# Top-32 attention into a mixture of experts: exponential before the mask, mask and product in one VectorE instruction

## The chip, the cores and the metric

The kernel runs on one NeuronCore of one Trainium2 chip. The metric is the device time of one launch in microseconds (us). A core has engines that run side by side, each with its own queue of instructions, executed in order: TensorE (PE in the profile; its weight loads are PEld), VectorE (DVE), ScalarE (ACT), GpSimd (POOL) and SyncE (SP, which issues transfers). An instruction that needs another engine's data waits on a semaphore, and all that stands behind it in its queue waits too.

## The reference

For 8 batches of 8 heads, 576 rows and head size 64, all in float32:

```python
scores = scale * np.matmul(q, k.transpose(0, 1, 3, 2))
kth = np.partition(scores, -32, axis=-1)[..., -32:-31]
scores = np.where(scores >= kth, scores, -1e9)
attn = np.exp(scores - scores.max(-1, keepdims=True))
attn = attn / (attn.sum(-1, keepdims=True) + 1e-9)
x = np.matmul(attn, v)
```

So each row of 576 scores keeps its 32 largest and takes a softmax over them. The result `x` (4608 rows of 512) goes through a mixture of 8 experts: each row is sent to one expert, two matrix products with a relu between them, and the result is scaled by the gate's probability.

## The kernel before

The attention is cut into 288 tiles of 128 rows by 576 scores: 32 pairs of heads, 9 tiles each. A loop over `i` runs one stage of several tiles in each pass, so that every engine has work of some tile. All engines get their instructions in the order in which the loop's Python code calls them; nothing reorders them later.

In pass `i` the stages of a tile `t` are these (the lag of a stage is the number of passes behind the tile's first stage on VectorE):

- TensorE computes the scores two passes ahead (`qk`), and ScalarE copies them from PSUM to SBUF as `Ssb` (`sevac`, L330).
- VectorE, lag 0: `subs` (L337), seven MAX8 over the seventh parts of a row, which gives 56 candidates. Lag 1: `chain` (L348 to L350), which takes the 24 largest of the candidates. `below` (L361) makes from the 24th a bound just under it.
- ScalarE, lag 3 (`KL + 1`): `sign` (L368) compares all scores with that bound. It writes the signs `K` and, with its accumulator, a sum `n` that tells how many scores lie above.
- GpSimd, lag 3: `pool_y` (L373) multiplies scores and signs to `y`, which hides the scores that are already counted.
- VectorE, lag 5 (`LT`): one MAX8 over the 576 values of `y` (L380) finds the next largest, and one scalar_tensor_tensor `jk` over 9 values (L381), by the count `n`, picks the 32nd largest, `kth`.
- VectorE, lag 5 (`LR`): `drop` (L387) writes `R`, which is 2 to the power 100 where a score is under `kth`, else 0.
- GpSimd, lag 6 (`LM`): `pool_m` (L392) subtracts `R` from the scores, giving `Sm`.
- ScalarE, lag 7 (`LE`): `expo` (L397) takes the exponential of `Sm` with the row's maximum subtracted, writes the probabilities `P` and their sum `den`.
- TensorE, lag 9 (`TL`): `trans` transposes `P`, ScalarE copies the result (`evac`), and TensorE multiplies with `v` (`av`).

VectorE's instructions of a pass come in three lists. `a_` holds the chain and `b_` the seven sub-maxima and the MAX8 over `y`; they are woven together. `c_` follows: `jk` (the pick), `below`, up to a few small instructions of routing and of the experts' scheduler ("side instructions" below; `small_` in the code), and `drop` last. TensorE fills its free time by a budget in the code (`STEP`, 3.2 us of estimated work a pass): what the attention leaves of it goes to matrix products of experts whose rows are ready. After the loop, from about 1100 us on, the remaining slots of the experts run alone.

GpSimd also does `small` (L356, the negated row maxima of three tiles), `fill` (L302, two copies each ninth pass), and the scattering transfers (L528, L718, L1088).

Of the kernel before, what the change touches and what calls it, by code (L numbers as in the profile page):

```python
# [19 lines left out]
TOPK = 32  # L20
NSUB = 7
CAP = 3.0
ME = 23
NB = 6
LX = 13
SN = 4
KB = 2
# [6 lines left out]
QL = 2  # L34
KW = 8
KL = 2
LT = KL + 3
LR = LT
LM = LR + 1
LE = LM + 1  # L40
TL = LE + 2
YB = 3
MB = 3
RB = 2
RL = (5, 6)
RX = (1, 3, 10, 12, 14)
HG = 2
# [6 lines left out]
QO = 0  # L54
# [7 lines left out]
BIG = float(2.0 ** 100)  # L62
# [7 lines left out]
def kernel(  # L70
# [35 lines left out]
    wk = att.enter_context(tc.tile_pool(name="wk", bufs=3))  # L106
# [5 lines left out]
    LD, PR, T = {}, {}, {}  # L112
    PAUSE = lambda: None

    def load(p, what, b=None):

        o = LD.setdefault(p, {})
        h0 = 2 * (p % HP)
        for nm in what:
            src = {"k": k, "q": q, "v": v}[nm]  # L120
            g = src[p // HP] if b is None else src[ds(b, 1)].rearrange("o h s d -> (o h) s d")
            t = ld.tile([128 if nm == "v" else 64, 2, D], FT, name=nm + "t", bufs=2 if nm == "v" else 1)
            m = ld.tile([128, 2, 4, D] if nm == "v" else [128, 4, 2, D], FT, name=nm + "m", bufs=2 if nm == "v" else 1)
# [25 lines left out]
    def fiota(name, shape, pattern, base, cm):  # L149
        t = const.tile(shape, FT, name=name)  # L150
        G.iota(t, pattern=pattern, base=base, channel_multiplier=cm, allow_small_or_imprecise_dtypes=True)
        return t

    i9s = fiota("i9s", [128, 9], [[2, 9]], S - 2 * TOPK, 0)
    ie = fiota("ie", [128, E], [[1, E]], -ZROW, 0)
    rev = fiota("rev", [128, E], [[-1, E]], E, 0)
    eoff = fiota("eoff", [128, E], [[LCAP, E]], -ZROW, 0)
# [15 lines left out]
    den = [const.tile([128, HP, 9], FT, name=f"den{i}") for i in range(2)]  # L173
    kth = const.tile([128, NT], FT, name="kth")
# [18 lines left out]
    x5 = const.tile([128, 5, XW], FT, name="x5")  # L193
# [25 lines left out]
    def bias_of(mw, mt, nb, bias):  # L219
        mf = wk.tile([128, nb, 5], FT, name="mf", bufs=1)  # L220
        G.memset(mf, 0.0)
        V.tensor_copy(mf[:, :, 0:4], mw[:, :, 0:8:2])
        V.tensor_copy(mf[:64, :, 4:5], mt[:, :, 0:1])
        nm = wk.tile([128, nb, 5], FT, name="nm", bufs=1)
        V.tensor_scalar(nm, mf, -1.0, 1.0, op0=OP.mult, op1=OP.add)
        tmp = wk.tile([128, nb, 5, E], FT, name="y", bufs=YB)
        bv = bias.rearrange("p b c e -> p (b c) e")
        tv = tmp.rearrange("p b c e -> p (b c) e")
        sh = [128, nb * 5, E]
        V.tensor_tensor(bv, mf.rearrange("p b c -> p (b c)")[:, :, None].to_broadcast(sh),  # L230
                        mbt[:, 1:2, :].to_broadcast(sh), op=OP.mult)
# [94 lines left out]
        T[i] = {"ps": ps}  # L326

    def sevac(i):
        T[i]["S"] = sb = wk.tile([128, S], FT, name="Ssb", bufs=LM + 1 + QL - QO)
        A.activation(sb.rearrange("p (a b) -> p a b", a=2), T[i]["ps"][:, :, :288], AF.Copy, scale=0.125)  # L330

    bnd = [(x * S) // NSUB for x in range(NSUB + 1)]
# [6 lines left out]
    def chain(i):  # L339
        if i % 3 == 0:  # L340
            T[i]["mg"] = wk.tile([128, 3, 32], FT, name="mg", bufs=5)
        else:
            T[i]["mg"] = T[i - 1]["mg"]
        m = T[i]["mg"][:, i % 3]
        c = T[i]["c"]
        c2 = wk.tile([128, NSUB * 8], FT, name="cand2", bufs=1)
        c3 = wk.tile([128, NSUB * 8], FT, name="cand3", bufs=1)
        return [lambda: V.max(m[:, 0:8], c), lambda: V.match_replace(c2, m[:, 0:8], c, -3e38),  # L348
                lambda: V.max(m[:, 8:16], c2), lambda: V.match_replace(c3, m[:, 8:16], c2, -3e38),
                lambda: V.max(m[:, 16:24], c3)]  # L350
# [6 lines left out]

    def below(i):
        t = T[i]
        t["n"] = wk.tile([128, 2], FT, name="n", bufs=NB)  # L360
        V.tensor_scalar(t["n"][:, 1:2], t["mg"][:, i % 3, 23:24], 1.0 - 2.0 ** -24, None, op0=OP.mult)  # L361

    def sign(i):


        t = T[i]
        t["K"] = wk.tile([128, S], BF, name="K", bufs=KB)
        A.activation(t["K"], t["S"], AF.Sign, scale=2.0 ** -24 - 1.0, bias=t["n"][:, 1:2], accum_out=t["n"][:, 0:1])  # L368

    def pool_y(i):  # L370
        t = T[i]
        t["y"] = wk.tile([128, S], FT, name="y", bufs=YB)
        G.tensor_tensor(t["y"], t["S"], t["K"], op=OP.mult)  # L373

    def top(i):
        t = T[i]
        y9 = t["mg"][:, i % 3, 23:32]
        jk = wk.tile([128, 9], FT, name="jk", bufs=2)
        kt = kth[:, i:i + 1]
        return [lambda: V.max(y9[:, 1:9], t["y"]),  # L380
                lambda: V.scalar_tensor_tensor(jk, i9s, t["n"][:, 0:1], y9, op0=OP.is_equal, op1=OP.mult,  # L381
                                               accum_out=kt)]

    def drop(i):
        t = T[i]
        t["R"] = wk.tile([128, S], BF, name="R", bufs=RB)
        V.tensor_scalar(t["R"], t["S"], kth[:, i:i + 1], BIG, op0=OP.is_lt, op1=OP.mult)  # L387

    def pool_m(i):
        t = T[i]  # L390
        t["Sm"] = wk.tile([128, S], FT, name="Sm", bufs=MB)
        G.tensor_tensor(t["Sm"], t["S"], t["R"], op=OP.subtract)  # L392

    def expo(i, dn):
        t = T[i]
        probs(i)
        A.activation(t["P"], t["Sm"], AF.Exp, bias=t["s"][:, i % 3:i % 3 + 1], accum_out=dn)  # L397

    def probs(i):

        c, h = divmod(i % 9, 2)
        T[i]["P"] = Pm[:, :S] if c == 4 else Pb[c % 2][:, h * S:h * S + S]
# [44 lines left out]
    spare = const.tile([1, 1], FT, name="spare")  # L447
# [383 lines left out]
    for x in range(QL):  # L831
        qk(x, 0, x, qbd[0])
        sevac(x)
    ok = lambda x: 0 <= x < NT
    PREP = dict(zip(PJ, "tkq"))
    spare_pe = 0.0
    LAST = NT + TL + LX
    rows_of = {}
    store = []
    for i in range(LAST):  # L840
# [19 lines left out]
        u = i - (KL + 1)  # L860
# [27 lines left out]
        if j == VJ and p < NPAIR:  # L888
            load(p, "v")
        b1, r = divmod(i - (TL + 2), 36)  # L890
        b1 -= 1
        if 0 <= b1 < B:
# [15 lines left out]
            if r == max(rl[1], rx[4]) + 2:  # L908
# [17 lines left out]
        while seen[0] and spare_pe > 0:  # L926
# [4 lines left out]
            c, f, new = moe[0]  # L931
# [11 lines left out]
        a_, b_, c_ = [], [], []  # L943
        if ok(i):
            b_ += subs(i)
        if ok(i - 1):
            a_ += chain(i - 1)
        if ok(i - LT):
            find, pick = top(i - LT)
            b_.insert(2, find)  # L950
            c_.append(pick)
        for x, f in enumerate(lo):
            b_.insert(LOP[x] if x < len(LOP) else len(b_), f)
        small_ = []
# [12 lines left out]
            small_.append(f)  # L967
        for x, f in enumerate(small_):
            c_.insert(2 * x, f)
        if ok(i - 1):  # L970
            c_.insert(min(len(c_), 1), lambda: below(i - 1))
        if ok(i - LR):
            c_.append(lambda: drop(i - LR))
        weave(a_, b_)
        for f in c_:
            f()

        if ok(i - LM):
            pool_m(i - LM)
        if ok(i - 2) and (i - 2) % 3 == 2:  # L980
            small(i - 4)
        if ok(i - (KL + 1)):
            pool_y(i - (KL + 1))
        if j == 3 and p < NPAIR:
            fill(p, qbd[p % 2])
        for x in puts:
# [18 lines left out]
    wk = att.enter_context(tc.tile_pool(name="tl", bufs=1))  # L1005
# [142 lines left out]
    wk = att.enter_context(tc.tile_pool(name="wkb", bufs=3))  # L1148
# [95 lines left out]
```

## Time and profile before

| | |
|---|---|
| median of 3 runs | 1347.67 us (1344.1 to 1347.98) |
| the profiled execution | 1348.8 us, of it a span of 1346.8 us from first to last instruction |
| VectorE busy | 1197.4 us (89%) |
| TensorE busy | 1222.6 us (91%), its weight loads 931.0 us |
| ScalarE busy | 1037.2 us (77%) |
| GpSimd busy | 861.6 us (64%) |
| mean granted TensorE clock | 0.97 of full speed |

Two shapes of view matter here. A timeline lists instructions with their start, how long they took, engine, line, output and inputs; the difference between two starts on one engine is what the first one costs there, which is often less than its duration, since the next instruction starts while the former still drains. A view by groups gives count, busy time and mean duration of one, and behind a second bar the idle time before them and what ended it.

### The profile page before, as it was taken

The numbers are of one execution on the slowest core, as the hardware profiler recorded it, in microseconds if no ns is written. First come the engines' busy times: TensorE is split into PE (matmuls) and PEld (weight loads), VectorE is DVE, ScalarE is ACT, GpSimd is POOL, SyncE is SP. The second block draws the span as 40 slices with busy tenths as digits, with TensorE's granted clock in tenths as the row PEclk, the third lists the DMA queues.
The fourth block names the chain that finished last, engine by engine and source line by source line (L and its number), as shares of the span: only waits on it lengthen the run. The fifth ranks groups of instructions, "written<-read, shape, count | busy, mean of one in ns | idle before, by whom it ended". The sixth has DMA issues, their size and how long they took to land. (4 is left out here: it accounts for less than half of the span.)

```text
span 1346.8 us, 29354 instructions
## 1 busy us (share of the span) xinstructions
PE 1222.6 (91%) x8197; PEld 931.0 (69%) x8197; DVE 1197.4 (89%) x6304; ACT 1037.2 (77%) x2309; POOL 861.6 (64%) x962
## 2 busy tenths in 40 slices
PE   6788888789999999999998999899989999999986
PEld 4666666576675766766766768577667557989985
DVE  3999999999999999999999999999999946776752
ACT  3889878878888888898898989798978744555542
POOL 2777778667788778777887787778878831011110
PEclk7999989799999999999999999999999999999998
DMA  4564334674547646545465565466545337766640
GB/s 116 148 178 112 81 81 116 173 181 120 146 116 199 161 112 186 151 104 158 126 195 151 122 177 150 100 167 182 149 113 143 117 101 242 245 207 232 232 169 14
DMA packets 206790, 201.08 MB, mean 149 GB/s; under 512 B 106221, under 2 KB 153325, under 8 KB 206608
## 3 DMA queue, kind: packets, MB, share of 16 engines
q1 hardware_dynamic: 200400, 179.48, 49.3%
q0 software_dynamic: 6208, 19.54, 4.0%
q8 instruction: 69, 1.13, 0.4%
q14 instruction: 113, 0.93, 0.2%
HBM read 118.63 MB, written 24.23 MB: 106 GB/s over the span
## 5 line engine op out<-in xcount | busy, mean ns | idle before, releaser
L392 POOL TENSOR_TENSOR Sm<-Ssb,R 128x576 f32<-128x576 f32 x288 | 370.2, 1285 | 202.2 <-DVE R L387 195.9
L337 DVE MAX8 cand<-Ssb 128x8 f32<-128x82 f32 (+1 forms) x2016 | 416.1, 230 | 21.6 <-ACT Ssb L330 21.5
L373 POOL TENSOR_TENSOR y<-Ssb,K 128x576 f32<-128x576 f32 x288 | 370.2, 1285 | 35.0 <-ACT K L368 33.3
L324 PE MATMUL S<-ks,qs 128*128 128x288 f32 x1024 | 229.4, 347 | 62.8 <-ACT Ssb L330 38.2
L397 ACT ACTIVATE P<-Sm,sm 128x576 f32<-128x576 f32 x256 | 200.3, 782 | 61.2 <-POOL Sm L392 59.8
L324 PEld LDWEIGHTS S<-ks,qs 128*128 128x128 f32 x1024 | 157.8, 194 | 128.5 <-ACT Ssb L330 72.8
L368 ACT ACTIVATE K<-Ssb,n 128x576 bf16<-128x576 f32 x288 | 227.3, 789 | 1.4 <-DVE n L361 1.4
L330 ACT ACTIVATE Ssb<-S 128x576 f32<-128x576 f32 x288 | 185.9, 645 | 39.1 <-PE S L324 39.0
L380 DVE MAX8 mg<-y 128x8 f32<-128x576 f32 x288 | 213.6, 742 | 0.2 <-POOL y L373 0.2
L416 ACT ACTIVATE PT<-T 128x640 f32<-128x640 f32 (+1 forms) x288 | 189.9, 659 | 4.2 <-PE T L408 4.2
L408 PE MATMUL T<-idf,P 128*128 128x128 f32 x1152 | 172.2, 277 | 1.9 <-ACT PT L416 1.9
L437 PE MATMUL X<-PT,vm 128*64 128x256 f32 (+1 forms) x1536 | 165.2, 345 | 4.6 <-issue 4.2
L387 DVE TENSOR_SCALAR R<-Ssb,kth 128x576 bf16<-128x576 f32 x288 | 154.4, 536 | 16.0 <-DVE n L361 0.4
L691 PE MATMUL E<-xgT,w1b 128*128 128x256 f32 x640 | 158.9, 391 | 2.9 <-ACT xgT L672 2.3
L703 PE MATMUL E<-w2b,hT 128*128 128x512 f32 x320 | 157.0, 605 | 1.8 <-ACT ot L713 1.8
L408 PEld LDWEIGHTS T<-idf,P 128*128 128x128 f32 x1152 | 136.8, 142 | 4.8 <-ACT PT L416 3.3
L691 PEld LDWEIGHTS E<-xgT,w1b 128*128 128x128 f32 x640 | 117.8, 193 | 28.2 <-issue 8.5
L437 PEld LDWEIGHTS X<-PT,vm 128*64 128x64 f32 x1536 | 81.9, 140 | 58.9 <-issue 29.5
L1088 POOL DMA_INDIRECT out_dram<-ot,tk x18 | 18.0, 1000 | 160.6 <-ACT ot L1087 160.6
L381 DVE SCALAR_TENSOR_TENSOR jk<-i9s,n,mg 128x9 f32<-128x9 f32 x288 | 111.5, 387 | 0.3
L703 PEld LDWEIGHTS E<-w2b,hT 128*128 128x128 f32 x320 | 54.0, 190 | 47.2 <-issue 42.3
L1066 PE MATMUL X<-xgh,w1h 128*128 128x256 f32 x216 | 62.9, 291 | 5.3 <-ACTq L1138 3.4
(206 smaller groups left out, 2439.9 us busy)
## 6 DMA issues: line engine op xcount, KB each, us to landing
w1b<-in_moe_w_dram SPq DMA_DIRECT2D x76, 512.0 KB, 7.6
w2b<-in_moe_w_dram SPq DMA_DIRECT2D x76, 512.0 KB, 5.6
ks<-st SPq DMA_DIRECT2D x64, 288.0 KB, 4.2
qs<-st SPq DMA_DIRECT2D x128, 144.0 KB, 4.0
ks<-st SPq DMA_DIRECT2D x62, 256.0 KB, 4.6
xg<-xs SPq DMA_DIRECT2D x19, 516.0 KB, 4.3
km<-in_k_dram SPq DMA_DIRECT2D x64, 128.0 KB, 4.7
qm<-in_q_dram SPq DMA_DIRECT2D x64, 128.0 KB, 3.3
```

The lines of the kernel that those rows point to most:

```text
L324: PE.matmul(ps[:, hf, u - a:v - a], l, d["ks"][:, x, h, u + o:v + o], start=(n == 0), stop=(n == len(terms) - 1), skip_group_check=(j == 8))
L337: return [lambda s=s: V.max(c[:, s * 8:s * 8 + 8], T[i]["S"][:, bnd[s]:bnd[s + 1]]) for s in range(NSUB)]
L368: A.activation(t["K"], t["S"], AF.Sign, scale=2.0 ** -24 - 1.0, bias=t["n"][:, 1:2], accum_out=t["n"][:, 0:1])
L373: G.tensor_tensor(t["y"], t["S"], t["K"], op=OP.mult)
L380: return [lambda: V.max(y9[:, 1:9], t["y"]), lambda: V.scalar_tensor_tensor(jk, i9s, t["n"][:, 0:1], y9, op0=OP.is_equal, op1=OP.mult, acc ...
L392: G.tensor_tensor(t["Sm"], t["S"], t["R"], op=OP.subtract)
L397: A.activation(t["P"], t["Sm"], AF.Exp, bias=t["s"][:, i % 3:i % 3 + 1], accum_out=dn)
L408: PE.transpose(T[i]["pt"][:, x, :], (Pm if c == 4 else Pb[c % 2])[:, h * 512 + x * 128:h * 512 + x * 128 + 128], idf)
L416: A.activation(o, T[i]["pt"][:, :n], AF.Copy)
L437: PE.matmul(o.rearrange("p (a b) -> p a b", a=2) if j < 8 else o, l, r, start=(c == 0), stop=(c == 4))
L691: PE.matmul(ps[:, f % 2], w1b[:, c, f * 128:(f + 1) * 128], xgT[:, c, :], start=(c == 0), stop=(c == KC - 1))
L703: PE.matmul(o["py"], hT[:, f, t * 128:(t + 1) * 128], w2b[:, f, :], start=(f == 0), stop=(f == FC - 1))
```

## The change

The exponential no longer waits for the mask. ScalarE takes it of all 576 scores (`expo`, into a new buffer `ex`, lag 6, without an accumulator). VectorE then makes the probabilities in one scalar_tensor_tensor over 576 values: (score >= kth) times `ex`, written to `P`, with the sum of the row in `den` (`keep`, lag 7, last in `c_`). `drop` on VectorE and `pool_m` on GpSimd are gone.

The pick of `kth` is done for three tiles at a time, each third pass: an is_equal and a product over 3 by 9 values and a reduction, each using the former's result. The bound `below` is made on GpSimd. `pool_y` has lag 4 instead of 3, and on GpSimd a one-element instruction `gate` stands ahead of it, which reads the `P` that `keep` wrote in the pass before. The pools change with it: the `Ssb` ring has 10 buffers instead of 9. The lag of the transposes stays 9.

```diff
-LT = KL + 3
-LR = LT
-LM = LR + 1
-LE = LM + 1
-TL = LE + 2
+LY = KL + 2
+LT = LY + 1
+LR = LT + 2
+LE = LR - 1
+TL = LR + 2
...
     def below(i):
         t = T[i]
-        V.tensor_scalar(t["n"][:, 1:2], t["mg"][:, i % 3, 23:24], 1.0 - 2.0 ** -24, None, op0=OP.mult)
+        x = i % 3
+        G.tensor_scalar(t["n"][:, 1, x:x + 1], t["mg"][:, x, 23:24], 1.0 - 2.0 ** -24, 1.0, op0=OP.mult, op1=OP.mult)
...
-                lambda: V.scalar_tensor_tensor(jk, i9s, t["n"][:, 0:1], y9, op0=OP.is_equal, op1=OP.mult,
-                                               accum_out=kt)]
-        V.tensor_scalar(t["R"], t["S"], kth[:, i:i + 1], BIG, op0=OP.is_lt, op1=OP.mult)
-        G.tensor_tensor(t["Sm"], t["S"], t["R"], op=OP.subtract)
-        A.activation(t["P"], t["Sm"], AF.Exp, bias=t["s"][:, i % 3:i % 3 + 1], accum_out=dn)
+        return [lambda: V.tensor_tensor(eq, i9s, n[:, :, None].to_broadcast([128, 3, 9]), op=OP.is_equal),
+                lambda: V.tensor_tensor(v, eq, t["mg"][:, :, 23:32], op=OP.mult),
+                lambda: V.tensor_reduce(kth[:, i - 2:i + 1], v, axis=AX.X, op=OP.add)]
+        A.activation(t["ex"], t["S"], AF.Exp, bias=t["s"][:, i % 3:i % 3 + 1])
+        V.scalar_tensor_tensor(t["P"], t["S"], kth[:, i:i + 1], t["ex"], op0=OP.is_ge, op1=OP.mult, accum_out=dn)
+    def gate(i):
+        G.tensor_scalar(spare[:, 0:1], T[i]["P"][0:1, 0:1], 1.0, 1.0, op0=OP.mult, op1=OP.mult)
...
+        if ok(i - 1 - LR):
+            gate(i - 1 - LR)
+        if ok(i - LY):
+            pool_y(i - LY)
+        if ok(i - 1):
+            below(i - 1)
         if ok(i - 2) and (i - 2) % 3 == 2:
             small(i - 4)
-        if ok(i - (KL + 1)):
-            pool_y(i - (KL + 1))
```

VectorE before, the end of one pass without side instructions and the start of the next (`R` is the mask, `jk` the pick, `n` the bound):

```order
L350 MAX mg<-cand_10138 128x8
L337 MAX cand<-Ssb 128x8 x2
L381 SCALAR_TENSOR_TENSOR jk,kth<-i9s,n,mg 128x9
L361 TENSOR_SCALAR n<-mg 128x1
L387 TENSOR_SCALAR R<-Ssb,kth 128x576
```

VectorE now, the end of a pass in which three thresholds are picked (the lines from eq to kth stand in each third pass only):

```order
L349 MAX mg<-cand_11446 128x8
L336 MAX cand<-Ssb 128x8 x2
L385 TENSOR_TENSOR eq<-i9s,n 128x27
L386 TENSOR_TENSOR jk<-eq,mg 128x27
L387 TENSOR_REDUCE kth<-jk 128x3
L398 SCALAR_TENSOR_TENSOR P_122,den_129<-Ssb,kth,ex 128x576
```

Two small instructions and a one-source mask became one two-source product in every pass, and three small ones that need each other in each third.

Where side instructions stand in a pass without a pick, VectorE had before (the `s_` names are the scheduler's):

```order
L590 TENSOR_TENSOR s_av<-base,roff 128x8
L361 TENSOR_SCALAR n<-mg 128x1
L381 SCALAR_TENSOR_TENSOR jk,kth<-i9s,n,mg 128x9
L591 SCALAR_TENSOR_TENSOR s_key<-s_av,rev 128x8
L592 MAX s_m_11211<-s_key 128x8
```

and now has:

```order
L595 TENSOR_TENSOR s_av<-base,roff 128x8
L596 SCALAR_TENSOR_TENSOR s_key<-s_av,rev 128x8
L597 MAX s_m_10858<-s_key 128x8
L598 TENSOR_SCALAR s_oh<-s_key,s_m_10858 128x8
L593 SCALAR_TENSOR_TENSOR s_jk,s_sc<-s_oh,s_av 128x8
```

The bound and the pick, which stood between the first side instruction and the one that needs it, are gone from there.

GpSimd in the middle of the attention, before:

```order
L356 TENSOR_SCALAR sm<-mg 128x3
L373 TENSOR_TENSOR y<-Ssb,K 128x576 [waits Activation_49]
L392 TENSOR_TENSOR Sm<-Ssb,R 128x576 [waits DVE_49]
L373 TENSOR_TENSOR y<-Ssb,K 128x576 [waits Activation_49]
L392 TENSOR_TENSOR Sm<-Ssb,R 128x576 [waits DVE_49]
```

and now:

```order
L402 TENSOR_SCALAR spare<-P_122 1x1 [waits DVE_49,Pool_49]
L374 TENSOR_TENSOR y<-Ssb,K 128x576 [waits Activation_49]
L361 TENSOR_SCALAR n<-mg 128x1 [waits DVE_49]
L402 TENSOR_SCALAR spare<-P_122 1x1 [waits DVE_49,Pool_49]
L374 TENSOR_TENSOR y<-Ssb,K 128x576 [waits Activation_49]
```

One of the two large GpSimd instructions of a pass is gone, and the other stands behind the wait for VectorE's product of the pass before.

## Rows read from the trace of the kernel before

**Rows 1.** Busy time of each engine in stretches of the span (us; in brackets the instructions), with granted clock, share of the transfer engines and GB/s.

```profile
400.00:600.00 200.00, 186.26 (x1223) 132.51 (x1219) 196.03 (x1129) 170.94 (x397) 155.66 (x163) 0.98 0.57 151
...
1080.00:1090.00 10.00, 9.75 (x59) 7.14 (x59) 1.32 (x5) 5.20 (x10) 1.49 (x2) 1.00 0.24 84
```

The columns behind the stretch and its length are PE, PEld, DVE, ACT and POOL.

**Rows 2.** Groups of VectorE instructions: count, busy us, mean ns of one, idle us before them and what ended it.

```profile
L337 DVE MAX8 cand<-Ssb 128x8 f32<-128x82 f32 x1440 | 328.5, 229 | 21.6 <-ACT Ssb L330 21.5
L380 DVE MAX8 mg<-y 128x8 f32<-128x576 f32 x288 | 213.6, 742 | 0.2 <-POOL y L373 0.2
L387 DVE TENSOR_SCALAR R<-Ssb,kth 128x576 bf16<-128x576 f32 x288 | 154.4, 536 | 16.0 <-DVE n L361 0.4
L381 DVE SCALAR_TENSOR_TENSOR jk<-i9s,n,mg 128x9 f32<-128x9 f32 x288 | 111.5, 387 | 0.3
```

**Rows 3.** All instructions of line 387 (the mask): shortest, median and longest in ns, and the starts of the first and the last in us.

```profile
L387 DVE TENSOR_SCALAR R<-Ssb,kth x288: 413/520/1501, 34.6 to 1080.3; 128x576 bf16<-128x576 f32 x144
```

**Rows 4.** VectorE's timeline over the end of one pass, a whole pass, and the end of the next (start us, us taken, instruction; in square brackets idle time before it).

```profile
300.47 0.21 DVE L381 SCALAR_TENSOR_TENSOR jk<-i9s,n,mg 128x9 f32<-128x9 f32 x1
300.61 0.08 DVE L381 DVE_READ_ACCUMULATOR jk<-i9s,n,mg 128x1 f32 x1
300.61 0.15 DVE L361 TENSOR_SCALAR n<-mg 128x1 f32<-128x1 f32 x1
300.80 0.52 DVE L387 TENSOR_SCALAR R<-Ssb,kth 128x576 bf16<-128x576 f32 x1
301.24 0.21 DVE L348 MAX8 mg<-cand 128x8 f32<-128x56 f32 x1
...
303.24 0.20 DVE L350 MAX8 mg<-cand 128x8 f32<-128x56 f32 x1
303.36 0.38 DVE L337 MAX8 cand<-Ssb 128x8 f32<-128x82 f32 x2
303.65 0.76 DVE L381 SCALAR_TENSOR_TENSOR jk<-i9s,n,mg 128x9 f32<-128x9 f32 x1
...
304.52 1.42 DVE L387 TENSOR_SCALAR R<-Ssb,kth 128x576 bf16<-128x576 f32 x1
```

**Rows 5.** GpSimd's timeline over the same stretch.

```profile
303.11 1.28 POOL L373 TENSOR_TENSOR y<-Ssb,K 128x576 f32<-128x576 f32 x1 [3.61 <-ACT K L368]
304.34 1.28 POOL L392 TENSOR_TENSOR Sm<-Ssb,R 128x576 f32<-128x576 f32 x1
```

**Rows 6.** Groups of VectorE instructions that run over one element at a time, in float32.

```profile
L1022 DVE TENSOR_TENSOR w2l<-w2b,w2h 128x1024 fp32r<-128x1024 f32 x36 | 44.0, 1224 | 17.8 <-PE X L1066 7.3 <-PE E L1066 6.8 <-ACT w2h L1021 3.1
L1069 DVE SCALAR_TENSOR_TENSOR hl<-X,hh 128x256 fp32r<-128x256 f32 x54 | 22.7, 421 | 34.9 <-ACT hh L1068 34.9
L591 DVE SCALAR_TENSOR_TENSOR s_key<-s_av,rev 128x8 f32<-128x8 f32 x20 | 3.2, 160 | 0.3
```

**Rows 7.** VectorE's timeline near the end: small instructions of which each needs the result of the one before.

```profile
1096.55 0.20 DVE L534 TENSOR_TENSOR r_l<-lgb,bias_all 128x40 f32<-128x40 f32 x1
1096.79 0.20 DVE L535 TENSOR_REDUCE r_mx<-r_l 128x5 f32<-128x40 f32 x1
1097.02 0.20 DVE L536 TENSOR_TENSOR r_z<-r_l,r_mx 128x40 f32<-128x40 f32 x1
```

**Rows 8.** VectorE's timeline over the end of one pass with side instructions, and over two side instructions of later passes.

```profile
1065.31 0.14 DVE L361 TENSOR_SCALAR n<-mg 128x1 f32<-128x1 f32 x1
1065.38 0.21 DVE L381 SCALAR_TENSOR_TENSOR jk<-i9s,n,mg 128x9 f32<-128x9 f32 x1
1065.52 0.08 DVE L381 DVE_READ_ACCUMULATOR jk<-i9s,n,mg 128x1 f32 x1
1065.52 0.15 DVE L591 SCALAR_TENSOR_TENSOR s_key<-s_av,rev 128x8 f32<-128x8 f32 x1
1065.71 0.17 DVE L592 MAX8 s_m<-s_key 128x8 f32<-128x8 f32 x1
...
1068.41 0.77 DVE L588 SCALAR_TENSOR_TENSOR s_jk<-s_oh,s_av 128x8 f32<-128x8 f32 x1
...
1072.27 1.15 DVE L612 SCALAR_TENSOR_TENSOR roff<-s_oh,s_sc,roff 128x8 f32<-128x8 f32 x1
```

**Rows 9.** GpSimd's timeline beside them.

```profile
1067.88 1.28 POOL L373 TENSOR_TENSOR y<-Ssb,K 128x576 f32<-128x576 f32 x1
...
1072.12 1.28 POOL L373 TENSOR_TENSOR y<-Ssb,K 128x576 f32<-128x576 f32 x1
```

**Rows 10.** Groups of GpSimd instructions that the change removes, adds to or moves past.

```profile
L392 POOL TENSOR_TENSOR Sm<-Ssb,R 128x576 f32<-128x576 f32 x288 | 370.2, 1285 | 202.2 <-DVE R L387 195.9 <-DMA ks<-st 4.3 <-DVE mg L348 1.8
L356 POOL TENSOR_SCALAR sm<-mg 128x3 f32<-128x3 f32 x96 | 19.4, 202 | 0.0
L302 POOL TENSOR_SCALAR qbd<-qs 128x64 fp32r<-128x64 f32 x64 | 15.6, 260 | 0.0
L454 POOL MEMSET spare<- 1x1 f32 x78 | 7.9, 101 | 0.4
```

**Rows 11.** Groups of ScalarE instructions of the exponential.

```profile
L397 ACT ACTIVATE P<-Sm,sm 128x576 f32<-128x576 f32 x256 | 200.3, 782 | 61.2 <-POOL Sm L392 59.8
L397 ACT ACTIVATION_READ_ACCUMULATOR P<-Sm,sm 128x1 f32 x256 | 51.1, 199 | 0.0
```

**Rows 12.** GpSimd's timeline at the end of the attention, its last subtraction.

```profile
1081.01 1.28 POOL L392 TENSOR_TENSOR Sm<-Ssb,R 128x576 f32<-128x576 f32 x1 [0.80 <-DVE R L387]
```

More of the change, by code (lines that the diff above doesn't have):

```diff
@@ L23 @@
 ME = 23
-NB = 6
+NB = 4
 LX = 13
@@ L36 @@
 KL = 2
-LT = KL + 3
-LR = LT
-LM = LR + 1
-LE = LM + 1
-TL = LE + 2
+LY = KL + 2
[3 more added lines that the diff above has]
+TL = LR + 2
 YB = 3
-MB = 3
-RB = 2
+XB = 3
 RL = (5, 6)
@@ L152, in fiota @@
         return t
-    i9s = fiota("i9s", [128, 9], [[2, 9]], S - 2 * TOPK, 0)
+    i9s = fiota("i9s", [128, 3, 9], [[0, 3], [2, 9]], S - 2 * TOPK, 0)
     ie = fiota("ie", [128, E], [[1, E]], -ZROW, 0)
@@ L225, in bias_of @@
         V.tensor_scalar(nm, mf, -1.0, 1.0, op0=OP.mult, op1=OP.add)
-        tmp = wk.tile([128, nb, 5, E], FT, name="y", bufs=YB)
+        tmp = x5[:, 0, :nb * 5 * E].rearrange("p (b c e) -> p b c e", b=nb, c=5)
         bv = bias.rearrange("p b c e -> p (b c) e")
@@ L328, in sevac @@
     def sevac(i):
-        T[i]["S"] = sb = wk.tile([128, S], FT, name="Ssb", bufs=LM + 1 + QL - QO)
+        T[i]["S"] = sb = wk.tile([128, S], FT, name="Ssb", bufs=LR + 1 + QL - QO)
         A.activation(sb.rearrange("p (a b) -> p a b", a=2), T[i]["ps"][:, :, :288], AF.Copy, scale=0.125)
@@ L359, in below @@
         t = T[i]
-        t["n"] = wk.tile([128, 2], FT, name="n", bufs=NB)
-        V.tensor_scalar(t["n"][:, 1:2], t["mg"][:, i % 3, 23:24], 1.0 - 2.0 ** -24, None, op0=OP.mult)
+        x = i % 3
+        t["n"] = T[i - 1]["n"] if x else wk.tile([128, 2, 3], FT, name="n", bufs=NB)
+        G.tensor_scalar(t["n"][:, 1, x:x + 1], t["mg"][:, x, 23:24], 1.0 - 2.0 ** -24, 1.0, op0=OP.mult, op1=OP.mult)
     def sign(i):
@@ L367, in sign @@
         t["K"] = wk.tile([128, S], BF, name="K", bufs=KB)
-        A.activation(t["K"], t["S"], AF.Sign, scale=2.0 ** -24 - 1.0, bias=t["n"][:, 1:2], accum_out=t["n"][:, 0:1])
+        A.activation(t["K"], t["S"], AF.Sign, scale=2.0 ** -24 - 1.0, bias=t["n"][:, 1, i % 3:i % 3 + 1],
+                     accum_out=t["n"][:, 0, i % 3:i % 3 + 1])
     def pool_y(i):
@@ L373, in pool_y, with find, pick, expo @@
         G.tensor_tensor(t["y"], t["S"], t["K"], op=OP.mult)
-    def top(i):
+    def find(i):
         t = T[i]
[L377 to L380, printed above, removed]
-                lambda: V.scalar_tensor_tensor(jk, i9s, t["n"][:, 0:1], y9, op0=OP.is_equal, op1=OP.mult,
-                                               accum_out=kt)]
-    def drop(i):
-        t = T[i]
-        t["R"] = wk.tile([128, S], BF, name="R", bufs=RB)
-        V.tensor_scalar(t["R"], t["S"], kth[:, i:i + 1], BIG, op0=OP.is_lt, op1=OP.mult)
-    def pool_m(i):
+        V.max(t["mg"][:, i % 3, 24:32], t["y"])
+    def pick(i):
+        t = T[i]
+        eq, v = (wk.tile([128, 3, 9], FT, name=nm, bufs=1) for nm in ("eq", "jk"))
+        n = t["n"][:, 0, :]
+        return [lambda: V.tensor_tensor(eq, i9s, n[:, :, None].to_broadcast([128, 3, 9]), op=OP.is_equal),
+                lambda: V.tensor_tensor(v, eq, t["mg"][:, :, 23:32], op=OP.mult),
+                lambda: V.tensor_reduce(kth[:, i - 2:i + 1], v, axis=AX.X, op=OP.add)]
+    def expo(i):
         t = T[i]
-        t["Sm"] = wk.tile([128, S], FT, name="Sm", bufs=MB)
-        G.tensor_tensor(t["Sm"], t["S"], t["R"], op=OP.subtract)
-    def expo(i, dn):
+        t["ex"] = wk.tile([128, S], FT, name="ex", bufs=XB)
+        A.activation(t["ex"], t["S"], AF.Exp, bias=t["s"][:, i % 3:i % 3 + 1])
+    def keep(i, dn):
         t = T[i]
         probs(i)
-        A.activation(t["P"], t["Sm"], AF.Exp, bias=t["s"][:, i % 3:i % 3 + 1], accum_out=dn)
+        V.scalar_tensor_tensor(t["P"], t["S"], kth[:, i:i + 1], t["ex"], op0=OP.is_ge, op1=OP.mult, accum_out=dn)
+    def gate(i):
+        G.tensor_scalar(spare[:, 0:1], T[i]["P"][0:1, 0:1], 1.0, 1.0, op0=OP.mult, op1=OP.mult)
     def probs(i):
@@ L868 @@
         if ok(u):
-            expo(u, den[(u // 36) % 2][:, (u // 9) % HP, u % 9:u % 9 + 1])
+            expo(u)
         while nxt:
@@ L948 @@
         if ok(i - LT):
-            find, pick = top(i - LT)
-            b_.insert(2, find)
-            c_.append(pick)
+            b_.insert(2, lambda: find(i - LT))
+            if (i - LT) % 3 == 2:
+                c_ += pick(i - LT)
         for x, f in enumerate(lo):
@@ L969 @@
             c_.insert(2 * x, f)
-        if ok(i - 1):
-            c_.insert(min(len(c_), 1), lambda: below(i - 1))
         if ok(i - LR):
-            c_.append(lambda: drop(i - LR))
+            u = i - LR
+            c_.append(lambda u=u: keep(u, den[(u // 36) % 2][:, (u // 9) % HP, u % 9:u % 9 + 1]))
         weave(a_, b_)
@@ L976 @@
             f()
-        if ok(i - LM):
-            pool_m(i - LM)
+        if ok(i - 1 - LR):
[4 more added lines that the diff above has]
+            below(i - 1)
         if ok(i - 2) and (i - 2) % 3 == 2:
             small(i - 4)
-        if ok(i - (KL + 1)):
-            pool_y(i - (KL + 1))
         if j == 3 and p < NPAIR:
```

## The prediction

> **What bounds the kernel now.** I read the busy shares by stretch first. From 60 to 1060 us every stretch looks like the one from 400 to 600 us [rows 1]: VectorE 196 of 200 us, TensorE 186, ScalarE 171, GpSimd 156. A modelled busy TensorE says little, so I looked next at what VectorE waits for. Its groups show hardly an idle time: 0.2 us before the MAX8 over `y`, and 21.6 us before the sub-maxima, most of it in the first passes; the 16 us before the mask are mostly its wait for the threshold that VectorE has just made [rows 2]. So the attention goes at the rate at which VectorE issues. From the first mask at 34.6 us to the last at 1080.3 us there are 287 steps [rows 3], so a pass takes 3.64 us, and what the change is worth is its sum on VectorE's queue, times 288. Since an instruction's successor starts before it has drained, I count from start to start. The 370 us that leave GpSimd [rows 10] and the accumulator reads that leave ScalarE [rows 11] are off that queue and count for nothing by themselves.
>
> The timeline of single passes gives the parts. From a chain's first MAX8 at 301.24 to the pick at 303.65 are 2.41 us, and the change leaves that part as it is. The four instructions of pick, read, bound and mask take from 300.47 to 301.24, 0.77 us, when nothing disturbs them [rows 4]. At 303.65 it is otherwise: the pick of 9 values takes 0.76 us and ends at 304.41, where GpSimd's product, begun at 303.11, ends at 304.39; the mask then takes 1.42 us and ends 0.32 us behind the end of GpSimd's next product at 305.62 [rows 4, 5]. So a VectorE instruction of this kind stands still while GpSimd's large one runs. The Trainium skill says the same (SBUF — State Buffer, "SBUF: two separate sides"): the two engines share one pair of ports, taken by whichever starts first and held for a whole instruction. It names VectorE instructions with two SBUF inputs and those in a two-port mode. By that rule the new product is as exposed as the old mask; the slower rival below prices this.
>
> **What VectorE loses.** 0.77 us a pass undisturbed. The pick's mean is 0.387 us where 0.21 us is undisturbed, the mask's mean is 0.536 us with a median of 0.520 us [rows 2 to 4]: 0.18 and 0.02 us of waiting. That makes 0.97 us. In the passes with side instructions (96 of 288 by the changed order) bound, pick and read hold the queue 0.21 us (1065.31 to 1065.52) [rows 8] and not 0.33 (300.47 to 300.80) [rows 4], which takes 0.04 off the mean: 0.93. I take 0.94 us, between the two; bounds 0.90 and 0.97. 288 x 0.94 = -271 us.
>
> **What it gains.** The product `keep`: no row has this shape. A scalar_tensor_tensor goes from 160 ns for 8 elements to 421 ns for 256, and a two-source product of 1024 takes 1224 ns [rows 6]; all three lie on 1.05 ns an element. The pick, the same instruction with a threshold pointer, costs 0.14 us start to start for 9 elements, and its accumulator read holds up nothing independent (300.61, where the bound starts at once) [rows 4]. So `keep` costs 0.14 + 567 x 0.00105 = 0.735 us: 288 x 0.735 = +212 us. Bounds: 0.68 us (the slope alone plus the least fixed part) and 0.81 us (its duration plus a read that counts).
>
> [...]
>
> The picks: three instructions of which each needs the former, and `keep` needs the last. Dependent ones are 0.23 to 0.24 us apart at 40 elements and 0.19 us at 8 [rows 7, 8], so 0.21 us at 27: 96 x 0.63 = +60 us. In the changed order 22 of the 96 picks have side instructions between them, which fill about half of these gaps, -7 us. Together +53 us; bounds 25 (all gaps filled by chance) and 65.
>
> Lost cover: today the bound and the pick stand between the first side instruction and its dependent (1065.31 to 1065.52, 0.21 us) [rows 8]. In 56 passes of the changed order with two or more side instructions and no pick these are now neighbours, and the dependent one waits some 0.12 us longer than its own cost: +7 us, between 0 and 12.
>
> Side instructions that GpSimd's product stops today: one took 0.77 us until a product from 1067.88 ended, another 1.15 us beside one from 1072.12 [rows 8, 9]. About ten such in the attention at 0.6 us are -6 us, between 0 and -15. In the changed order `y` starts when the former `keep` is done. It takes 1.29 us and ends over a microsecond before the 2.41 us of MAX8 do, which were never slowed in the rows.
>
> **Where GpSimd's small instructions fall.** The bound waits for the chain's last MAX8. That ends at 303.44 in the pass shown [rows 4]; some 0.1 us later GpSimd starts it, for about 0.2 us as its like, `sm` [rows 10]. `keep` would start at 303.65 and needs 0.14 us itself before it streams, so the bound hides behind its start. In each third pass `sm` follows directly, 0.2 us more, and there the pick's first instruction loses about 0.09 us: 74 plain picks, +7 us. Bounds: 0, and 0.2 us in every pass, +58 us.
>
> **The end.** After the last pick the subtraction (1.28 us) [rows 12] and the exponential with its read (0.78 + 0.2 us) [rows 11] leave the chain, `keep` and two later passes join it. TensorE is busy 9.75 of the 10 us from 1080 on [rows 1], with experts' work, so I take -2 us, from 0 to -5.
>
> The sum: -271 + 212 + 53 + 7 - 6 + 7 - 2 = 0. Against the profiled execution's 1348.8 us that is 1349 us; the median of the runs stands 1.1 us lower, and the small terms lean more below than above their values, so I say 1347 us. No wait that the change adds stands on VectorE's path: `ex` is ready a pass ahead; the scores' copy now waits for `keep` of the pass before, but is needed two passes later; `gate` holds only GpSimd, whose work falls to about 1.9 us a pass.
>
> **Rivals.** *Faster (the cover costs nothing).* If the picks' gaps are filled (25), the lost cover is 0, the side instructions give 15 and the end 5, GpSimd's small ones nothing: -271 + 212 + 25 - 15 - 5 = -54 us at the far end, half of that likelier: 1322 us. For it: in passes without side instructions the present tail is the most disturbed, and these are more than half. Against it: the dependent gaps of [rows 7]. TensorE's 186 of 200 us [rows 1] would cap it.
>
> *Slower (GpSimd's small instructions hold the two-source product).* The place is the end of a pass: bound, `sm` and in each ninth pass two fills of 0.26 us [rows 10] run just where `keep` and the picks want to start. At 0.1 us in each pass the price is +22 us over what I counted, 1370 us; it decides from 0.02 us a pass on. Against it: the start-up of `keep` as counted. Beside it goes the possibility that an instruction over two SBUF sources with an accumulator streams slower than the rows for each apart.
>
> *A new wait.* `keep` waits for ScalarE, the sub-maxima for copies that wait for `keep`: one stop of 2 us in each tenth pass is +58 us. The groups show next to no such stops now, and the slack is over a pass.
>
> **How the numbers follow.** Forecast (sum within 10 us of the profile) 0.50, own range 1337 to 1357; faster rival 0.23; slower rival 0.19; new wait 0.08. A difference under 0.3% (4 us) can't be told from none. Of the forecast's half I put 0.16 under 1343.6 us, 0.22 within, 0.12 above 1351.7. The faster rival gives 0.21 below and 0.02 within, the slower 0.03 within and 0.16 above, the wait 0.08 split as 0.01, 0.01, 0.06, which I round to faster 0.38, same 0.28, slower 0.34. The range cuts a tenth off each side: 1328 to 1366 us.
>
> **What would show it.** `keep` with a mean near 0.76 us and its successor 0.73 to 0.74 us behind its start; three pick instructions some 0.2 us apart; no VectorE instruction of the tail that ends with GpSimd's `y`; the period between two `keep` near 3.64 us. Wrong: `keep` with a tail of long durations that end with GpSimd's small instructions, or idle time before `keep` put down to ScalarE, or TensorE with no gap left.

## The result and the profile after

The changed kernel takes 1358.59 us (median of 4 runs, 1358.19 to 1361.28), the kernel before 1347.83 us beside it: ratio 1.0087, 95% interval 1.0069 to 1.0104. It is slower, by 11 us, where no clear change was forecast. The profiled execution has a span of 1357.1 us.

The busy shares by stretch hardly move on the three loaded engines, and GpSimd's falls, as [rows 1] can be compared with (columns as there):

```profile
400.00:600.00 200.00, 186.99 (x1227) 133.44 (x1229) 196.51 (x1068) 169.63 (x348) 110.39 (x216) 0.99 0.59 152
```

VectorE was busy 196.0 us in this stretch and now 196.5: it is still what sets the rate. Over the whole attention the MAX8 over `y` stands once in each pass. These are all of line 378, shortest, median and longest in ns, and the first and last start in us:

```profile
L378 DVE MAX8 mg<-y x288: 731/742/762, 32.6 to 1085.8; 128x8 f32<-128x576 f32 x144
```

and before:

```profile
L380 DVE MAX8 mg<-y x288: 730/742/761, 32.5 to 1078.7; 128x8 f32<-128x576 f32 x144
```

So each of the 287 steps now lasts 3.670 us in the mean instead of 3.645. That is 7 us of the 11. The rest comes behind it: from the last of these to the end of the span are 271.3 us instead of 268.1.

The VectorE groups that replace those of [rows 2] (count, busy us, mean ns, idle us before and what ended it):

```profile
L398 DVE SCALAR_TENSOR_TENSOR P<-Ssb,kth,ex 128x576 f32<-128x576 f32 x256 | 213.3, 833 | 10.8 <-ACT ex L392 0.5 <-ACT K L368 0.4
...
L385 DVE TENSOR_TENSOR eq<-i9s,n 128x27 f32<-128x27 f32 x96 | 25.0, 261 | 0.0
...
L386 DVE TENSOR_TENSOR jk<-eq,mg 128x27 f32<-128x27 f32 x96 | 18.0, 187 | 2.7
L387 DVE TENSOR_REDUCE kth<-jk 128x3 f32<-128x27 f32 x96 | 17.4, 181 | 2.6
```

Almost nothing is lost to waiting for other engines' data: 10.8 us ahead of the product, most of it for the threshold. So the time has to be in what VectorE itself issues. Its timeline over the end of a pass with picks, and the end of the next without:

```profile
300.43 0.39 DVE L336 MAX8 cand<-Ssb 128x8 f32<-128x82 f32 x2
300.72 0.18 DVE L385 TENSOR_TENSOR eq<-i9s,n 128x27 f32<-128x27 f32 x1
300.93 0.19 DVE L386 TENSOR_TENSOR jk<-eq,mg 128x27 f32<-128x27 f32 x1
301.15 0.18 DVE L387 TENSOR_REDUCE kth<-jk 128x3 f32<-128x27 f32 x1
301.46 0.82 DVE L398 SCALAR_TENSOR_TENSOR P<-Ssb,kth,ex 128x576 f32<-128x576 f32 x1
302.21 0.08 DVE L398 DVE_READ_ACCUMULATOR P<-Ssb,kth,ex 128x1 f32 x1
302.21 0.21 DVE L347 MAX8 mg<-cand 128x8 f32<-128x56 f32 x1
...
304.33 0.38 DVE L336 MAX8 cand<-Ssb 128x8 f32<-128x82 f32 x2
304.62 0.80 DVE L398 SCALAR_TENSOR_TENSOR P<-Ssb,kth,ex 128x576 f32<-128x576 f32 x1
305.35 0.08 DVE L398 DVE_READ_ACCUMULATOR P<-Ssb,kth,ex 128x1 f32 x1
```

The product costs 0.73 to 0.75 us start to start, as forecast. The picks, undisturbed, cost 0.21, 0.22 and 0.31 us, together 0.74 us and not 0.63. Passes behind a transfer that GpSimd issues look different. VectorE there:

```profile
522.45 1.24 DVE L398 SCALAR_TENSOR_TENSOR P<-Ssb,kth,ex 128x576 f32<-128x576 f32 x1
...
526.04 1.02 DVE L385 TENSOR_TENSOR eq<-i9s,n 128x27 f32<-128x27 f32 x1
```

and GpSimd beside it (`spare` with L402 is the gate, `n` the bound):

```profile
519.57 0.59 POOL L361 TENSOR_SCALAR n<-mg 128x1 f32<-128x1 f32 x1
520.44 1.03 POOL L533 DMA_INDIRECT xs<-x,dest  x1 [0.27 <-DVE cand L336]
521.48 0.09 POOL L459 MEMSET spare<- 1x1 f32 x1
521.66 0.18 POOL L402 TENSOR_SCALAR spare<-P 1x1 f32<-1x1 f32 x1
521.81 1.27 POOL L374 TENSOR_TENSOR y<-Ssb,K 128x576 f32<-128x576 f32 x1
523.16 0.59 POOL L361 TENSOR_SCALAR n<-mg 128x1 f32<-128x1 f32 x1
...
525.75 1.27 POOL L374 TENSOR_TENSOR y<-Ssb,K 128x576 f32<-128x576 f32 x1
```

In a pass without a transfer GpSimd has:

```profile
302.60 1.27 POOL L374 TENSOR_TENSOR y<-Ssb,K 128x576 f32<-128x576 f32 x1
304.50 0.19 POOL L361 TENSOR_SCALAR n<-mg 128x1 f32<-128x1 f32 x1 [0.64 <-DVE mg L349]
```

The transfer's issue stands ahead of the gate on GpSimd's queue, so `y` starts over a microsecond late and ends at 523.08. The product that began at 522.45 gets on only then and ends at 523.69; the first pick, from 526.04, stands still in the same way beside the `y` from 525.75. Below, this is called a collision. The bound `n`, 0.19 us elsewhere, is held by the product in turn. It also makes the transfer late: it waits for a MAX8 near the end of the pass (L349), here it ends at 520.16, and the transfer stands behind it in the queue.

Adding the starts of all VectorE instructions between 60 and 1060 us, start to start, gives the mean cost of a pass by part (us):

| part | before | after |
|---|---|---|
| MAX8 and MATCH_REPLACE | 2.421 | 2.425 |
| pick, accumulator read, bound, mask | 0.936 | |
| product `keep` | | 0.755 |
| picks (three instructions each third pass) | | 0.254 |
| side instructions | 0.294 | 0.255 |
| all | 3.651 | 3.689 |

The two windows hold 274 and 271 passes, not quite the same ones, so their sums differ by more than the steps above. Over the same 279 steps of both, up to the last MAX8 over `y`, the sums are 3.642 and 3.673 us, and no part differs from the table by more than 0.025 us.

So three parts differ from the forecast's terms: the picks (0.254 against 53 us / 288 = 0.184), the product's mean (0.755 against 0.735), and the side instructions, which became cheaper by 0.04 us a pass.

### The profile page after: what moved, and what is told of

The parts are those of the page before. It is cut to its first block, busy times and chain, and to the rows that moved or that the text cites. A ratio compares the mean times of both kernels' runs of the same rounds, so it can differ in the third digit from the quotient of the medians.

```text
span 1357.1 us, 29327 instructions
## 1 busy us (share of the span) xinstructions
PE 1222.5 (90%) x8197; PEld 929.6 (69%) x8197; DVE 1205.9 (89%) x6016; ACT 1022.8 (75%) x2021; POOL 634.5 (47%) x1250
## 5 line engine op out<-in xcount | busy, mean ns | idle before, releaser
L374 POOL TENSOR_TENSOR y<-Ssb,K 128x576 f32<-128x576 f32 x288 | 367.2, 1275 | 2.5 <-ACT K L368 2.1
L323 PE MATMUL S<-ks,qs 128*128 128x288 f32 x1024 | 226.5, 344 | 68.0 <-ACT Ssb L329 44.3
L368 ACT ACTIVATE K<-Ssb,n 128x576 bf16<-128x576 f32 x288 | 226.1, 785 | 58.9 <-POOL y L374 58.4
L392 ACT ACTIVATE ex<-Ssb,sm 128x576 f32<-128x576 f32 x288 | 223.4, 776 | 0.0
L398 DVE SCALAR_TENSOR_TENSOR P<-Ssb,kth,ex 128x576 f32<-128x576 f32 x256 | 213.3, 833 | 10.8 <-ACT ex L392 0.5
L361 POOL TENSOR_SCALAR n<-mg 128x1 f32<-128x1 f32 x288 | 69.5, 241 | 199.1 <-DVE mg L349 193.4
L402 POOL TENSOR_SCALAR spare<-P 1x1 f32<-1x1 f32 x256 | 47.2, 184 | 224.7 <-DVE mg L347 206.6
```

What stands on the lines that cost most here:

```text
L323: PE.matmul(ps[:, hf, u - a:v - a], l, d["ks"][:, x, h, u + o:v + o], start=(n == 0), stop=(n == len(terms) - 1), skip_group_check=(j == 8))
L392: A.activation(t["ex"], t["S"], AF.Exp, bias=t["s"][:, i % 3:i % 3 + 1])
L398: V.scalar_tensor_tensor(t["P"], t["S"], kth[:, i:i + 1], t["ex"], op0=OP.is_ge, op1=OP.mult, accum_out=dn)
```

## The experiments

Three theories. A: the loss is the gaps between the picks, where each waits for the one before, at the end of a pass with nothing to fill them. B: it is GpSimd's `y`, late behind transfers, that stops two-source instructions of VectorE. C: it is the price of the two-source product as such. All runs take the changed kernel and alter one or two things. The reference point is its 1358.6 us; the kernel before took 1347.8 to 1348.0 us beside each series, so times of different series can be compared.

### The picks among the sub-maxima

```diff
-            if (i - LT) % 3 == 2:
-                c_ += pick(i - LT)
...
-        weave(a_, b_)
+        m_ = []
+        weave([lambda f=f: m_.append(f) for f in a_], [lambda f=f: m_.append(f) for f in b_])
+        if ok(i - LT) and (i - LT) % 3 == 2:
+            for f, back in zip(pick(i - LT), (5, 4, 3)):
+                m_.insert(len(m_) - back if ok(i) else len(m_), f)
+        for f in m_:
+            f()
```

> The changed kernel with the three pick instructions set among the last sub-maxima of the same pass, each separated from the next by MAX8s, instead of one behind the other ahead of the product. Theory A (what the change lost is the picks' dependent gaps at the end of each third pass: 0.76 us a pick on the changed kernel's timeline, of which about 0.3 us are the instructions' own cost): 96 x 0.45 = 43 us less, 1310 to 1325 us, and the product some 0.1 us behind the last MAX8 in every pass. Theory B (what it lost is GpSimd's y, started late in passes with a transfer to issue, that stops the picks and the product): the picks stand nearer to y, so no gain or a loss, 1350 to 1370 us. Theory C (the two-source product itself is what costs): no change, 1355 to 1361 us.

Measured: 1336.15 us, ratio to the kernel before 0.9922 (0.9904 to 0.9941). 22 us less than the changed kernel, half of what theory A said, and the opposite of B's sign; C's range is missed too. The trace says why only half. Picks fell from 0.254 to 0.121 us a pass, which is 38 us. The product went up, to 0.784 us: of the 288, 31 last over 0.95 us instead of 15. Here is one, on VectorE:

```profile
510.93 1.23 DVE L398 SCALAR_TENSOR_TENSOR P<-Ssb,kth,ex 128x576 f32<-128x576 f32 x1
```

and on GpSimd:

```profile
508.91 1.03 POOL L533 DMA_INDIRECT xs<-x,dest  x1 [0.27 <-DVE cand L336]
509.94 0.09 POOL L459 MEMSET spare<- 1x1 f32 x1
510.12 0.18 POOL L402 TENSOR_SCALAR spare<-P 1x1 f32<-1x1 f32 x1
510.27 1.27 POOL L374 TENSOR_TENSOR y<-Ssb,K 128x576 f32<-128x576 f32 x1
```

30 of these 31 have the same history: a transfer, then `y`, then the product that stands still until 511.54 and ends 0.62 us later. So A is right in kind, and B's mechanism is there too and took part of the gain: what had stopped the picks now stops the product.

### One threshold a pass

```diff
-            if (i - LT) % 3 == 2:
-                c_ += pick(i - LT)
+            c_ += pick(i - LT)
```

with `pick` as the scalar_tensor_tensor over 9 values of the kernel before.

> The changed kernel with one part undone: the threshold is picked for each tile in its own pass by the one scalar_tensor_tensor of the kernel before, and the product still comes two passes behind it, so it waits for no pick of its own pass. Theory A: 0.14 us in each pass instead of 0.76 us in each third, which is 0.11 us a pass or 31 us less: 1322 to 1335 us. Theory B: a two-source instruction now stands at the end of every pass and not of each third, so the collisions with a late y stay or grow: 1350 to 1365 us. Theory C: 1355 to 1361 us.

Measured: 1341.81 us, ratio 0.996 (0.9946 to 0.9973), 17 us less than the changed kernel. It lies between A's range and B's. The groups of product and pick:

```profile
L397 DVE SCALAR_TENSOR_TENSOR P<-Ssb,kth,ex 128x576 f32<-128x576 f32 x256 | 207.5, 810 | 2.8 <-ACT ex L391 2.8
...
L385 DVE SCALAR_TENSOR_TENSOR jk<-i9s,n,mg 128x9 f32<-128x9 f32 x288 | 79.4, 276 | 0.1
```

The pick costs 0.202 us a pass where 0.137 us is its median: it now stands where the late `y` falls, and is held instead of the product, which is clean (0.738 us, none over 0.95 us). Undoing the picking by threes alone turns the change into a small gain: as it stood in the change, that part cost 17 us.

### No gate

```diff
-        if ok(i - 1 - LR):
-            gate(i - 1 - LR)
```

> The changed kernel without the one-element GpSimd instruction that makes y wait for the product of the pass before. Theory B says that y runs as early as ScalarE's signs let it and then across the product of the same pass: some products last 1 to 2 us, the kernel is slower, 1365 to 1400 us. If the gate itself delays y into the next product (it is queued behind transfers), it is faster, 1340 to 1355 us. Theories A and C speak of VectorE alone and say no more than 5 us either way.

Measured: 1449.8 us, ratio 1.076 (1.0739 to 1.0782): 91 us slower than with the gate, more than B's upper end. 83 of the 288 products last over 0.95 us. The groups of product and `y`:

```profile
L398 DVE SCALAR_TENSOR_TENSOR P<-Ssb,kth,ex 128x576 f32<-128x576 f32 x256 | 260.6, 1018 | 10.8 <-ACT ex L392 0.5 <-DVE roff L617 0.4
```

```profile
L374 POOL TENSOR_TENSOR y<-Ssb,K 128x576 f32<-128x576 f32 x288 | 410.9, 1427 | 11.5 <-ACT K L368 2.4
```

Both engines now lose: `y` grew from 1275 to 1427 ns in the mean and the product from 833 to 1018 ns. Without the one-element gate the change costs 102 us against the kernel before, with it 11 us: theory B's collision is dear wherever it happens.

### The bound back on VectorE

```diff
-        G.tensor_scalar(t["n"][:, 1, x:x + 1], t["mg"][:, x, 23:24], 1.0 - 2.0 ** -24, 1.0, op0=OP.mult, op1=OP.mult)
+        V.tensor_scalar(t["n"][:, 1, x:x + 1], t["mg"][:, x, 23:24], 1.0 - 2.0 ** -24, None, op0=OP.mult)
...
-        if ok(i - 1):
-            below(i - 1)
+            c_.insert(min(len(c_), 1), lambda: below(i - 1))
```

> The changed kernel with the bound (one multiplication of one column) back on VectorE. The rival of the prediction (GpSimd's small instructions at the end of a pass hold the picks and the product): its cost of 0.06 us a pass comes on VectorE, +17 us, but the collisions with it go; if they cost 0.1 us a pass, 1345 us, else 1370 to 1378 us. Theories A and B: 1370 to 1378 us.

Measured: 1356.73 us, ratio 1.0072 (1.0055 to 1.009), 2 us less than the changed kernel. It lies between the two outcomes expected (1345 us, and 1370 to 1378), so neither came true. On VectorE the bound costs 0.069 us a pass, 20 us; the first pick instruction falls from 0.094 to 0.046 us a pass and the product from 0.755 to 0.737, which gives nearly all of it back. The time alone doesn't tell whether the bound itself had collided or whether it had delayed what stands behind it. The trace speaks for the second: a transfer's issue now starts at 518.74 us, right behind the `y` from 517.29 to 518.58, and between 60 and 1060 us no product lasts over 0.95 us. The next run tests it with the bound on GpSimd.

### GpSimd's order

```diff
         if ok(i - LY):
             pool_y(i - LY)
-        if ok(i - 1):
-            below(i - 1)
         if ok(i - 2) and (i - 2) % 3 == 2:
             small(i - 4)
+        for f in sends:
+            f()
+        for x in puts:
+            x[0] -= 1
+        while puts and puts[0][0] <= 0:
+            puts.popleft()[1]()
         if j == 3 and p < NPAIR:
             fill(p, qbd[p % 2])
-        for x in puts:
-            x[0] -= 1
-        while puts and puts[0][0] <= 0:
-            puts.popleft()[1]()
+        if ok(i - 1):
+            below(i - 1)
```

`sends` are the scattering transfers of rows, taken out of `c_` by lines that are not shown here.

> The changed kernel with only GpSimd's order inside a pass changed: behind the gate come y, the negated maxima, the transfers to issue, the fills, and the bound last, so that no transfer stands between a product and the next y. Theory B in the form that the traces now give (27 late y after a transfer stopped 15 products and 12 picks): the product's mean falls from 0.755 to 0.74 us a pass and the first pick instruction's from 0.28 to about 0.15 us, together 0.05 us a pass, 10 to 16 us less: 1342 to 1349 us. Theory A alone (only the picks' gaps): 1356 to 1361 us.

Measured: 1344.77 us, ratio 0.9978 (0.9968 to 0.9988): 14 us less than the changed kernel, inside theory B's range and outside A's. The groups:

```profile
L398 DVE SCALAR_TENSOR_TENSOR P<-Ssb,kth,ex 128x576 f32<-128x576 f32 x256 | 208.2, 813 | 12.9 <-ACT ex L392 2.5 <-ACT K L368 0.4
...
L386 DVE TENSOR_TENSOR jk<-eq,mg 128x27 f32<-128x27 f32 x96 | 18.0, 187 | 2.7
L387 DVE TENSOR_REDUCE kth<-jk 128x3 f32<-128x27 f32 x96 | 17.4, 181 | 2.6
L385 DVE TENSOR_TENSOR eq<-i9s,n 128x27 f32<-128x27 f32 x96 | 16.2, 169 | 0.0
```

Only the collisions went: `eq` is at 169 ns instead of 261, the product at 813 instead of 833, while the two dependent picks are as before to the nanosecond. The bound is still on GpSimd here, at the end of each pass, so it was not the bound itself that collided. It had stood ahead of the transfers and made them late, and they, ahead of the gate, had made `y` late. Since the run moves transfers, fills and bound together, it doesn't share the 14 us out among them. Of the 15 products that its expectation puts behind transfers, 13 are; the other two are those of the end, discussed below.

### Both

This run has the edit of the woven picks and that of GpSimd's order.

> The picks woven among the sub-maxima as in the second run before this, and GpSimd's order as in the run beside this. If both causes are separate, the gains add: picks 0.10 us a pass, product 0.735, side instructions 0.24, MAX8s 2.425, so 3.50 us a pass instead of 3.60 with the weave alone: 1302 to 1316 us. If the late y is hidden by something else: 1330 to 1336 us as with the weave alone.

Measured: 1319.16 us, ratio 0.9792 (0.9775 to 0.9809). That is 39 us less than the changed kernel; the two gains apart were 22 and 14 us. So they about add up; the 3 us beyond are no more than runs of one kernel differ by. The weave no longer hands its collisions to the product: 3 of the 288 last over 0.95 us instead of 31. The time stayed 3 us above the range given. The timeline of a pass with picks:

```profile
515.03 0.17 DVE L385 TENSOR_TENSOR eq<-i9s,n 128x27 f32<-128x27 f32 x1
515.12 0.23 DVE L336 MAX8 cand<-Ssb 128x8 f32<-128x83 f32 x1
515.28 0.16 DVE L386 TENSOR_TENSOR jk<-eq,mg 128x27 f32<-128x27 f32 x1
515.37 0.23 DVE L336 MAX8 cand<-Ssb 128x8 f32<-128x82 f32 x1
515.52 0.16 DVE L387 TENSOR_REDUCE kth<-jk 128x3 f32<-128x27 f32 x1
515.60 0.20 DVE L349 MAX8 mg<-cand 128x8 f32<-128x56 f32 x1
515.73 0.37 DVE L336 MAX8 cand<-Ssb 128x8 f32<-128x82 f32 x2
516.02 0.80 DVE L398 SCALAR_TENSOR_TENSOR P<-Ssb,kth,ex 128x576 f32<-128x576 f32 x1
```

The three instructions cost 0.09, 0.09 and 0.08 us here, 0.26 us in place of 0.74, with the same instructions and the same data. The MAX8s between them are needed anyway.

### One threshold a pass, with the order

This run has the edit of one threshold a pass and that of GpSimd's order.

> The threshold picked for each tile in its own pass, and GpSimd's order changed. The pick there cost 0.20 us a pass with 0.14 undisturbed, the product was clean: the order returns at most 0.06 us a pass, 10 to 18 us: 1324 to 1333 us. If picking three at a time is worth something where it is woven, this stays 8 us or more behind the woven kernel with the same order.

Measured: 1324.35 us, ratio 0.9827 (0.981 to 0.9844). As expected for the order's part (17 us less than without it). The woven picks by threes are 5 us faster still. That is less than the 8 us named beforehand, and the two intervals just don't overlap: picking by threes is worth something once its gaps are filled, but little.

## Why the prediction was wrong

The time lay inside the range, but the forecast of no change was wrong: the loss of 11 us is clear. Step by step:

- *VectorE sets the rate; what leaves GpSimd and ScalarE counts for nothing by itself.* Right for the 287 steps. GpSimd lost 227 us of busy time (861.6 to 634.5 us) and the time went up. At the end TensorE decides (last point).
- *What VectorE loses, 0.94 us a pass.* Right: 0.936 us by the sum over all starts.
- *The product at 0.735 us.* Right as a price: median 0.737 us. The mean was 0.755 us, by 13 collisions in 271 passes, each behind a transfer. The product lasts 0.80 us and its successor starts 0.73 us behind its start. The Trainium skill (VectorE: DVE Perf Modes, "The DRAIN you can't avoid") has the next instruction wait until the pipe is empty, but lets one that nothing holds start earlier, and this trace agrees with the latter.
- *The picks, +53 us.* This is the term that was most mis-sized: 0.254 us a pass, +73 us. Of three plain gaps taken at 0.21 us the last was 0.31 us, and the first pick ran into a late `y` in 12 of 91 cases. With GpSimd's order changed, which removed these collisions, the picks still cost 0.221 us a pass, 64 us: of the 20 us too many about half are the gaps and half the late `y`.
- *`y` "ends over a microsecond before the 2.41 us of MAX8 do".* This step failed. In passes without a transfer `y` is clear of the product, by 0.75 us (302.60 to 303.87 us, with the product at 304.62). Behind a transfer it is not. The argument had named what is queued behind the gate, but not what is queued ahead of it: 40 scattering transfers and 20 of the results, of about 1 us each, and ahead of these the bound, which waits for the end of the pass. Theory B's run shows this order to cost 14 us.
- *GpSimd's small instructions, +7 us, and the slower rival built on them.* The place was right, the mechanism wrong. `keep` is stopped by `y`, not by the bound, `sm` or the fills: all 15 products of over 0.95 us end 0.62 us behind the end of a `y`. The bound matters by delaying the transfers.
- *Side instructions: +7 us for lost cover, -6 us for collisions gone.* Measured about -12 us together. The traces hold the same 387 of them in the same 279 steps: the kinds that became dearer add up to 1.7 us, those that became cheaper to 14 us. By this count the lost cover was taken too high and the collisions too low.
- *The end, -2 us.* Wrong in sign: +3 us. VectorE's part came as said: from the last MAX8 over `y` until the rows can be scaled are 4.2 us (1085.84 to 1090.06) instead of 7.1 (1078.70 to 1085.83). But TensorE, with the same matrix products in the same order, was 9.9 us later than before by then, and VectorE 7.1 us. Before:

```profile
1067.34 3.72 PE L691 MATMUL E<-xgT,w1b 128*128 128x256 f32 x16 [0.84 <-ACT xgT L672]
...
1094.27 0.77 PE L491 MATMUL X<-idf,x 128*128 128x128 f32 x5 [0.63 <-ACT x L483]
```

and now, with ScalarE's sign in the last line:

```profile
1078.04 3.72 PE L696 MATMUL E<-xgT,w1b 128*128 128x256 f32 x16 [2.35 <-ACT xgT L677]
...
1104.16 0.77 PE L496 MATMUL X<-idf,x 128*128 128x128 f32 x5 [0.63 <-ACT x L488]
```

```profile
1076.25 0.78 ACT L368 ACTIVATE K<-Ssb,n 128x576 bf16<-128x576 f32 x1 [1.37 <-POOL y L374]
```

The longer wait at 1078.04 us is for a copy that stood on ScalarE behind this sign, and the sign waited for a `y`. Such waits are new: 58.4 us of ScalarE's idle time in all, and still 29.5 us without the gate. So `gate` and the later `y` do not hold "only GpSimd", as the prediction had it, though VectorE shows no wait from it. How much of the end's 3 us is this one wait, no run tells. Two products, from 1082.10 and 1084.30 us, also collide and last 1.60 us each, in passes that have no more sub-maxima to cover `y`; they lie in the last steps, ahead of the last MAX8 over `y`.

Together: over the same 279 steps the parts add up to -262 + 212 + 70 - 12 = +8 us; the first steps give back 1.5 us and the end adds 3 us, which is the 10 us between the two profiled spans. That the time stayed inside the range is partly luck: without the 12 us that the side instructions gave back, it would have been about 1371 us.

What the change lost it lost to the order of instructions, not to its arithmetic: with picks and transfers moved, the same instructions run 2.1% below the kernel before.

## What to carry to other kernels

On an engine that is issuing all the time, price a small instruction by whether its successor needs it: the same three instructions cost 0.74 us in a row and 0.26 us between independent ones. Where two engines exclude each other, follow the queue of the one that must keep clear, with everything that may stand ahead of its gate and what that waits for, through the passes that differ from the usual one. A part of a change that brings a loss can be undone alone, so measure the parts before giving up the whole.

## What the runs showed of the hardware that was not expected

- The product waits longer for a threshold from a reduction than the other dependent instructions do for theirs: 0.31 us from start to start (301.15 to 301.46) against 0.21 and 0.22 us, in the changed kernel and with GpSimd's order changed alike (median 0.314 us in both). The product also waits for ScalarE's exponential, which may add a step to its wait; that was not tried.
- When a VectorE product and GpSimd's `y` overlap, the later one stands still and not both go slower: the product that began at 510.93 us ended 0.62 us behind the end of `y`, about the time that its 576 elements need at the 1.05 ns of [rows 6]. It goes the other way round too. Without the gate a `y` that began just behind a product took 1.79 us instead of 1.28:

```profile
599.93 0.79 DVE L398 SCALAR_TENSOR_TENSOR P<-Ssb,kth,ex 128x576 f32<-128x576 f32 x1
```

```profile
600.07 1.79 POOL L374 TENSOR_TENSOR y<-Ssb,K 128x576 f32<-128x576 f32 x1
```

- GpSimd's bound of one column takes 0.19 us alone. In the changed kernel 30 of the 288 lasted 0.58 to 0.98 us, each beside a product and ending some 0.05 us behind it: even an instruction as small as this is held.
- The issue of a transfer on GpSimd is held too. In the changed kernel the eight scattering or result transfers that began 0.11 to 0.16 us behind the start of a product took 1.57 to 1.64 us; the usual is about 1.0 us.
